# A state-space scan with a gated feed-forward: four turns a tile, moments by pairs, C in its own buffer, GpSimd out of the last tiles

## The chip, the cores and the metric

The kernel runs on one core of one Trainium2 chip. The metric is the device time of one execution in microseconds (us); it was measured three times for the kernel before the change (median 190.08 us), and once more in the execution that the profiler recorded.

Engines are called PE (matrix products, TensorE), DVE (VectorE), ACT (ScalarE), POOL (GpSimd) and SP (SyncE, which here only issues transfers). Each executes its own instructions in the order in which they were written, and waits for others through semaphores.

## The reference

The input x has 2048 tokens of 448 numbers. Both branches work on its normalized rows; the first is a linear recurrence over the tokens with 448 complex states, the second a gated feed-forward layer with 1792 hidden units.

```python
def _A_ref(x, Lambda_re, Lambda_im, B_re, B_im, C_re, C_im, log_dt, Dskip):
    ...
    Lam_bar = jnp.exp(dt * Lam)
    B_bar = ((Lam_bar - 1.0) / Lam)[:, None] * Bmat
    Bu = jnp.einsum("bld,pd->blp", x + 0j, B_bar)
    ...
    for t in range(L):
        h = Lam_bar[None, :] * h + Bu[:, t, :]
        hs.append(h)
    ...
    y = 2.0 * jnp.einsum("blp,dp->bld", hseq, Cmat).real + x * Dskip[None, None, :]
    return y

def _B_ref(x, w_gate, w_up, w_down):
    g = jnp.einsum("bsd,df->bsf", x, w_gate)
    u = jnp.einsum("bsd,df->bsf", x, w_up)
    h = _sigmoid(g) * u
    return jnp.einsum("bsf,fd->bsd", h, w_down)

x = A_x
xn = _layernorm(x, axis=-1)
s = _A_ref(xn, A_Lambda_re, A_Lambda_im, A_B_re, A_B_im, A_C_re, A_C_im, A_log_dt, A_Dskip)
g = _silu(_B_ref(xn, B_w_gate, B_w_up, B_w_down))
return x + s * g
```

## The kernel before

The tokens are cut into four chunks (c = 0 to 3) of 512, each of four tiles of 128 tokens (j = 0 to 3, numbered t = 4c + j over all). A chunk needs its normalized rows `xn[c % 3]` (tokens on the partitions) and their transposed form `xnT[c]` (features on the partitions). The 448 features make three blocks of 128 and one of 64. The last block stands twice in `xnT`, on the upper and on the lower 64 partitions, because the kernel runs nearly all its products on half of the rows at a time (`HALF`), an upper and a lower one side by side.

*Normalization.* `ln_stats` (L208) computes a tile's mean and variance on DVE; `ln_var` (L232) writes variance plus epsilon to `ve` on DVE; `ln_pow` (L239) raises it to the power -1/2 on POOL, giving `rsd`; `ln_norm` (L259) writes the rows. Chunk 0 is transposed by PE (`turn_twice`, L196: three turns of 128 columns, one of the last 128 columns, and one of the last 64 into the upper half of the same place). The later chunks are transposed by DMA (`ln_turn`, L272), after `ln_twice` has copied the last 64 columns once more behind the row (columns 448 to 512). Chunk 1's four tiles share one `ln_var` and one `ln_pow`.

*Order of the work.* `keep_order` binds every engine to the written order. The stream of PE is written by `emit_line`: lists of pairs of units, each pair a `duo` (L1053). A unit is either one block of the feed-forward (gate and up, `gu_unit`) or one block of the state input (`bu_unit`). A duo first does the upper half of its first unit beside the lower half of its second, then the other two halves. The table `beside`, filled by `at(c, ft, cost, fn)`, says what is written behind which half; `pieces` and `fill` spread the scan's DVE work over the stream by costs.

*The word between the halves.* A sum that goes on in the other half of the rows must not overtake the products of the first half. Class `Sum` (L505) therefore puts an empty instruction into POOL's queue, which waits for the last product of the one half, and on which the first product of the other half waits:

```python
            if self.half not in (None, half):
                word = pool.nop()
                tc.add_manual_dep(word.ins, self.ins.ins.name, SYNC, reason="the other half's last product")
                tc.add_manual_dep(m.ins, word.ins.name, SYNC, reason="the other half's last product")
```

A duo has four of these words (three with the short last block of the state input), all ahead of or among its second half's products. The profile shows them as L513 of POOL's sequencer (POOLq).

*The start.* A burst of empty products (`warm`) comes first; then chunk 0's tiles 0 and 1 are normalized and turned, the first feed-forward blocks are begun, tiles 2 and 3 follow. ACT computes sines and cosines of the scan's rotations, POOL mirrors them (`emit_neg`, `emit_mirror`, four times four instructions). The duo (4, 5) is the first that has words.

*C.* `load_wd_c` (L158), at place (0, 7), issues on SP the load of the down-projection weights `wd` and four loads of the output matrix C (`c_re`, `c_im`, into the buffers that `b_re`, `b_im` had). `emit_c_turn` (L170) transposes them by DMA, four times each; `emit_c` (L458) mixes them into `ct` with ACT and DVE during chunk 1's down-projection.

*The end.* After the last down-projection, `emit_y` and `emit_fin` do the last chunk's tiles in the order 0, 2, 1, 3, tile 3 in two halves of columns. A tile's output is x + (y + skip) * g. `emit_rest_of` (L843) prepares x + skip * g in float32, on DVE for even tiles and on POOL for odd ones; `emit_fin` adds y * g to it, on POOL for tile 1.

Of the kernel before, what the change touches and what calls it, by code (L numbers as in the profile page):

```python
# [63 lines left out]
def kernel(  # L64
# [93 lines left out]
    def load_wd_c():  # L158
        sync.dma_start(out=wd[:], in_=B_w_down.rearrange("(ft p) d -> p ft d", p=P))

        for nm in ("c_re", "c_im"):
            raw[nm] = w.tile([P, KT, DP], BF16, name=nm, tag="raw" + nm[1:])
            ctr[nm] = w.tile([P, KT, D], BF16, name="t" + nm, tag="tc" + nm[1:])
        for nm, mat, other in (("c_re", A_C_re, A_C_im), ("c_im", A_C_im, A_C_re)):

            for f0, m, c0 in ((0, mat, 0), (D, other, 384)):
                sync.dma_start(out=raw[nm][0:CP, :, f0:f0 + D - c0],
                               in_=m[:, c0:D].rearrange("(kt p) f -> p kt f", p=CP))
# [100 lines left out]
    def ln_turn(c, j):  # L269
        xb, cols = xn[c % 3], slice(j * P, (j + 1) * P)  # L270
        if c > 0:
            sync.dma_start_transpose(out=xnT[c][:, 0:KT, cols], in_=xb[:, j, :])  # L272
            return
        turn_twice(tps[j % 2], xb[:, j, :], P)

    def ln_twice(c, copy):
        copy(out=xn[c % 3][:, :, D:DP], in_=xn[c % 3][:, :, 384:D])
        for j in range(TPC):
            ln_turn(c, j)
# [178 lines left out]
    def emit_c(i):  # L458
# [9 lines left out]
        if not c_room:  # L468
            for nm in ("raw_re", "raw_im"):
                both = []  # L470
                c_room.extend((nm, both, k) for k in range(2))
                if nm == "raw_re":
                    c_room.extend((None, None, None) for _ in range(2))
            c_room.append((None, None, None))
# [280 lines left out]
    def emit_downs(c):  # L755
# [27 lines left out]
        for q in range(TPC):  # L783
            beside_each(*(v[q * FT:(q + 1) * FT] for v in line))
            if q >= 2:
                empty(q - 2)
                empty(q)
                if c == NCH - 1:
                    if q == 2:

                        pieces.pop(0)[1]()
                    emit_gate()
                    emit_gate()
# [11 lines left out]
    def y_ops(c, j, rows, d0=0, d1=D):  # L805
        sl = slice(j * P, (j + 1) * P)
        o = []
# [33 lines left out]
    rests, room_of_rests = {}, {}  # L841

    def emit_rest_of(c, j):  # L843

        eng = dve if j % 2 == 0 else pool
        t = op_.tile([P, D], BF16, name="t_g", tag="zb", bufs=4)
        eng.tensor_tensor(out=t[:], in0=xn[c % 3][:, j, 0:D], in1=gs[c][:, j, :], op=ALU.mult)  # L847
        if not rests:
            for k, nm in ((0, "raw_re"), (2, "raw_im")):
                both = w.tile([P, 2, D], FP32, name="t_x", tag=nm)  # L850
                room_of_rests.update({k: both[:, 0, :], k + 1: both[:, 1, :]})
        rests[j] = room_of_rests[j]
        eng.tensor_tensor(out=rests[j], in0=t[:], in1=x_t[c][:, j, :], op=ALU.add)  # L853

    def emit_y(c, j, d0=0, d1=D):
        ops = y_ops(c, j, slice(0, P), d0, d1)
# [5 lines left out]
    def emit_fin(c, j, d0=0, d1=D):  # L862
# [7 lines left out]
        (pool if j == 1 else dve).tensor_tensor(out=o[:, d0:d1], in0=sg[:, d0:d1], in1=rests[j][:, d0:d1], op=ALU.add)  # L870
# [75 lines left out]
    emit_angles()  # L946
    ln_mean(2, 1)
# [4 lines left out]
    warm(4)  # L952
# [60 lines left out]
    while due:  # L1013
        emit_mul()
    ln_stats(TPC)
    ln_stats(TPC + 1)
# [6 lines left out]
    for j in range(2, TPC):  # L1023
        at(0, 5, 0.8, lambda j=j: ln_stats(TPC + j))
    at(0, 5, 0.1, lambda: ln_var(TPC, TPC))
    at(0, 7, 0.0, lambda: ln_pow(TPC, TPC))
    for j in range(TPC):
        at(0, 7, 0.41, lambda j=j: ln_norm(1, j))
    at(0, 7, 0.2, lambda: ln_twice(1, dve.tensor_copy))
# [5 lines left out]
    at(0, 7, 0.0, load_wd_c)  # L1035
    for place, nm in (((1, 0), "c_re"), ((1, 1), "c_im")):
# [95 lines left out]
```

## Time and profile before

| | us |
|---|---|
| three timed runs | 188.74, 190.08, 190.25 (median 190.08) |
| the profiled execution, its own time | 188.31 |
| its span, first to last instruction | 186.5 |
| PE busy | 180.0 |
| DVE busy | 164.2 |
| ACT busy | 114.0 |
| POOL busy | 34.2 |
| first down-projection product of chunks 0, 1, 2, 3 | 42.78, 86.35, 128.94, 165.47 |
| last product | 181.9 |
| last DVE instruction ends | 183.97 |

Times in the prediction are microseconds from the span's start. The profile names an instruction by its engine, its line in the kernel, and the tiles it writes and reads (out<-in). Busy time of PE contains overlap, since products are pipelined: two half-row products run side by side, and a pair takes 0.215 us. What an engine waited for is inferred from semaphore events. PEld is the loading of weights into PE, which runs beside the products.

### The profile page before, as it was taken

The page shows a single profiled execution, that of the slowest core. Times are in us where ns is not written, and L with a number is a line of the kernel's source. Part 1 is how long each engine was busy: PE and PEld are TensorE (multiplying, and loading weights), DVE is VectorE, ACT ScalarE, POOL GpSimd, SP SyncE. Part 2 cuts the span into 40 slices and gives each one's busy share as a digit, 9 for nine tenths or more (in the row PEclk, how much of TensorE's full clock was granted, in tenths as well). Part 3 has the DMA queues.
Part 4 walks back from the last instruction along what each step waited for, and adds up shares of the span by engine and source line. Part 5 has one row for each costly group of instructions (what it writes and reads, how often), then busy time and mean ns, then how long its engine had stood idle before and what let it go on. Part 6 is the DMA issues. An engine that isn't in the chain of part 4 may idle for free.

```text
span 186.5 us, 4470 instructions
## 1 busy us (share of the span) xinstructions
PE 180.0 (97%) x1699; PEld 96.1 (52%) x1699; DVE 164.2 (88%) x326; ACT 114.0 (61%) x236; POOL 34.2 (18%) x71
## 2 busy tenths in 40 slices
PE   7999999999998999999999999999999999999990
PEld 6666444445553444655554445545554445655560
DVE  4779979999997979999999999699999999699584
ACT  3969857989549975997557757057038657061300
POOL 4699467402000000004000000000000000000092
PEclk9999999999999999999999999999999999999997
DMA  5999955894434113011140010020000010020102
GB/s 152 326 323 222 241 143 96 239 295 94 94 74 91 28 32 98 0 54 51 32 80 20 18 28 0 4 98 2 4 11 18 4 23 10 0 87 14 28 25 74
DMA packets 27659, 15.07 MB, mean 81 GB/s; under 512 B 16243, under 2 KB 27638, under 8 KB 27638
## 3 DMA queue, kind: packets, MB, share of 16 engines
q1 hardware_dynamic: 27632, 14.79, 32.7%
q8 instruction: 13, 0.21, 0.5%
q14 instruction: 8, 0.07, 0.1%
q10 hardware_dynamic: 6, 0.00, 0.0%
HBM read 8.49 MB, written 1.84 MB: 55 GB/s over the span
## 4 chain that ended last, share of the span: by engine, by line
PE 71%; SPq 8%; DMA 6%; issue 6%; POOL 2%; DVE 2%; ACT 1%; POOLq 0%; ACTq 0%
PE g_ps L511 18%; PE u_ps L511 16%; PE d_ps L511 14%; PE y_ps L511 8%; PE bu L511 6%; SPq L171 5%; DMA c_re<-in_A_C_im_dram 5%; SPq L272 2%; PE warm_ps L194 2%; PE g_ps L703 2%; DMA tc_im<-c_im 2%; PE u_ps L703 2%; DVE o_l L870 1%; POOL t_g L847 1%; POOL t_x L853 1%
## 5 line engine op out<-in xcount | busy, mean ns | idle before, releaser
L511 PE MATMUL u_ps<-xnT,wu 64*128 64x512 bf16 x312 | 66.9, 376 | 0.5 <-ACT zb L771 0.5
L511 PE MATMUL g_ps<-xnT,wg 64*128 64x512 bf16 x312 | 59.0, 376 | 0.0
L741 ACT ACTIVATE sig<-g_ps 128x512 bf16<-128x512 f32 x52 | 29.2, 598 | 28.0 <-PE g_ps L511 27.9
L511 PE MATMUL bu<-xnT,bT 64*128 64x512 bf16 x196 | 45.5, 376 | 0.0
L511 PE MATMUL d_ps<-wd,hF 64*128 64x448 bf16 x448 | 43.9, 349 | 0.0
L511 PEld LDWEIGHTS <-hF 64*128 64x128 bf16 x448 | 25.0, 94 | 18.0 <-POOLq L513 0.7
L511 PEld LDWEIGHTS <-wu 64*128 64x128 bf16 x312 | 24.0, 94 | 19.2 <-POOLq L513 1.6
L511 PEld LDWEIGHTS <-wg 64*128 64x128 bf16 x312 | 21.1, 94 | 18.3 <-POOLq L513 1.8
L741 ACT CAST ub<-u_ps 128x512 bf16<-128x512 f32 x52 | 29.2, 607 | 0.0
L511 PEld LDWEIGHTS <-bT 64*128 64x128 bf16 x196 | 17.8, 94 | 11.5 <-issue 0.8
L590 DVE TENSOR_TENSOR_SCAN wv<-r_col,st,ta 128x512 bf16<-128x512 f32 x18 | 22.6, 1275 | 0.1
L511 PE MATMUL y_ps<-ct,h 64*128 64x448 bf16 (+2 forms) x203 | 22.5, 343 | 0.0
L738 DVE TENSOR_TENSOR hF<-sig,ub 128x512 bf16<-128x512 bf16 x52 | 20.8, 415 | 0.9 <-ACT ub L741 0.8
L511 PE MATMUL g_ps<-xnT,wt 64*128 64x512 bf16 x52 | 19.6, 376 | 0.0
L511 PE MATMUL u_ps<-xnT,wt 64*128 64x512 bf16 x52 | 19.6, 376 | 0.0
L847 POOL TENSOR_TENSOR t_g<-xn,g_t 128x448 bf16<-128x448 bf16 x2 | 2.5, 1225 | 89.5 <-ACT g_t L765 89.5
L511 PEld LDWEIGHTS <-h 64*128 64x128 bf16 (+1 forms) x203 | 13.3, 95 | 8.3 <-issue 0.4
L571 ACT CAST bus<-bu 128x512 bf16<-128x512 f32 x24 | 14.4, 602 | 2.9 <-PE bu L511 2.9
L240 POOL TENSOR_TENSOR rsd<-ve,mhalf 128x1 f32<-128x1 f32 (+1 forms) x7 | 6.3, 903 | 49.7 <-PE u_ps L511 46.5
L769 ACT ACTIVATE sigd<-d_ps 128x448 bf16<-128x448 f32 x12 | 6.6, 550 | 12.4 <-PE d_ps L511 12.4
L511 PEld LDWEIGHTS <-wt 64*128 64x128 bf16 x104 | 9.8, 94 | 5.6
L834 DVE TENSOR_TENSOR o_t<-y_ps,xn 128x448 bf16<-128x448 f32 x12 | 6.9, 618 | 3.5 <-PE y_ps L511 3.4
(154 smaller groups left out, 235.3 us busy)
## 6 DMA issues: line engine op xcount, KB each, us to landing
wd<-in_B_w_down_dram SPq DMA_DIRECT2D x1, 1568.0 KB, 8.2
x<-in_A_x_dram SPq DMA_DIRECT2D x3, 448.0 KB
out_dram<-o_t SPq DMA_DIRECT2D x6, 224.0 KB, 2.1
wg<-in_B_w_gate_dram SPq DMA_DIRECT2D x2, 384.0 KB, 4.1
wu<-in_B_w_up_dram SPq DMA_DIRECT2D x2, 384.0 KB, 5.1
wg<-in_B_w_gate_dram SPq DMA_DIRECT2D x1, 576.0 KB, 5.7
wu<-in_B_w_up_dram SPq DMA_DIRECT2D x1, 576.0 KB, 6.7
bsw<-bus SPq DMA_DIRECT2D x8, 64.0 KB, 2.0
```

Source lines behind the costliest of these rows:

```text
L171: sync.dma_start_transpose(out=ctr[nm][:, :, kt * CP:(kt + 1) * CP], in_=raw[nm][0:CP, kt, :])
L194: pe.matmul(warm_ps[:], lhsT=ident[:], rhs=ident[:], start=True, stop=True)
L240: pool.tensor_tensor(out=rsd[:, t:t + n, :], in0=ve[:, t:t + n, :], in1=mhalf[:, 0:n, :], op=ALU.pow)
L511: m = pe.matmul(self.t[:, n0:n1], lhsT=lhsT, rhs=rhs, start=self.done == 1, stop=self.done == self.n)
L571: empty = [lambda cc=cc: act.copy(out=bus[:, cc, :], in_=pst[cc][:]) for cc in range(2)]
L590: dve.tensor_tensor_scan(out=T["wv"][:, cc, :], data0=rb, data1=T["ta"][:, cc, :], initial=(0.0 if c == 0 else st[pt][:, cc, :]), op0=mul, ...
L703: pe.matmul(t[:, n0:n1], lhsT=wm[:, kt, f0:f1], rhs=xnT[c][:, kt, n0:n1], start=(first and kt == 0), stop=(not first and kt == 2))
L738: dve.tensor_tensor(out=h[:], in0=sig[:], in1=ub[:], op=ALU.mult)
L741: u.empty = [lambda: act.activation(sig[:], gt[:], ACT.Sigmoid), lambda: act.copy(out=ub[:], in_=ut[:])]
L769: act.activation(sigd[:], ds[j][:], ACT.Sigmoid)
L834: dve.tensor_tensor(out=o[:, i, :], in0=ys[c, j + 2 * i][:], in1=xb[:, i, :], op=ALU.add)
L847: eng.tensor_tensor(out=t[:], in0=xn[c % 3][:, j, 0:D], in1=gs[c][:, j, :], op=ALU.mult)
```

## The change

- Chunk 0's rows get their last 64 columns copied behind the row as well (on DVE for tiles 0 and 1, on POOL for tiles 2 and 3), and PE turns a tile in four turns of 128 columns instead of five turns. The empty products around them become 2 and 5 instead of 4.
- Chunk 1's moments, `ve` and `rsd` are computed by pairs of tiles, written between the first four products hF (`emit_mul`), ahead of the duo (4, 5). The normalization of chunk 1 and its DMA turns go, by pairs, from place (0, 7) to (0, 5).
- `c_re` gets a buffer of its own and is loaded ahead of chunk 1's turns; `c_im` takes the buffer of `b_re` and is loaded between the two pairs of turns. `wd` follows at (0, 6). The turns of C go from (1, 0) and (1, 1) to (0, 12) and (1, 0).
- For the last chunk's odd tiles POOL prepares nothing: PE adds the skip rows to the sum by one product with the identity, and DVE adds x itself. POOL's addition for tile 1 goes to DVE.

In the built program the instructions of POOL stand in this order afterwards: the mirrors, then the two `rsd` of 128x2, then the first words of L513, then the scan's constants. Before, the mirrors are followed by words and constants, and `rsd` of 128x4 comes behind the words of the duos (4, 5) and (6, 7).

```diff
-    def load_wd_c():
-        sync.dma_start(out=wd[:], in_=B_w_down.rearrange("(ft p) d -> p ft d", p=P))
...
+    def load_c(nm, mat, other):
+        raw[nm] = w.tile([P, KT, DP], BF16, name=nm, tag=("raw_c", "raw_re")[nm == "c_im"])
+        ctr[nm] = w.tile([P, KT, D], BF16, name="t" + nm, tag="tc" + nm[1:])
+
+        for f0, m, c0 in ((0, mat, 0), (D, other, 384)):
+            sync.dma_start(out=raw[nm][0:CP, :, f0:f0 + D - c0],
+                           in_=m[:, c0:D].rearrange("(kt p) f -> p kt f", p=CP))
...
-        turn_twice(tps[j % 2], xb[:, j, :], P)
-
-    def ln_twice(c, copy):
-        copy(out=xn[c % 3][:, :, D:DP], in_=xn[c % 3][:, :, 384:D])
-        for j in range(TPC):
+        (dve if j < 2 else pool).tensor_copy(out=xb[:, j, D:DP], in_=xb[:, j, 384:D])
+        for kt in range(KT):
+            pe.transpose(tps[j % 2][:, kt, :], xb[:, j, kt * P:(kt + 1) * P], ident[:])
+
+    def ln_twice(c, copy, j0=0, j1=TPC):
+        copy(out=xn[c % 3][:, j0:j1, D:DP], in_=xn[c % 3][:, j0:j1, 384:D])
+        for j in range(j0, j1):
             ln_turn(c, j)
...
-    def y_ops(c, j, rows, d0=0, d1=D):
+    def y_ops(c, j, rows, d0=0, d1=D, skipped=False):
         sl = slice(j * P, (j + 1) * P)
-        o = []
+        o = [(ident[rows, :], xn[c % 3][rows, j, d0:d1], d0, d1)] if skipped else []
...
     def emit_rest_of(c, j):
-
-        eng = dve if j % 2 == 0 else pool
+        if j % 2:
+            return
...
     def emit_y(c, j, d0=0, d1=D):
-        ops = y_ops(c, j, slice(0, P), d0, d1)
+        ops = y_ops(c, j, slice(0, P), d0, d1, j not in rests)
...
-        (pool if j == 1 else dve).tensor_tensor(out=o[:, d0:d1], in0=sg[:, d0:d1], in1=rests[j][:, d0:d1], op=ALU.add)
+        also = rests[j] if j in rests else x_t[c][:, j, :]
+        dve.tensor_tensor(out=o[:, d0:d1], in0=sg[:, d0:d1], in1=also[:, d0:d1], op=ALU.add)
...
     ln_turn(0, 0)
     emit_vecs()
     emit_angles()
+    warm(2)
...
-    warm(4)
+    warm(5)
...
-    while due:
+    emit_mul()
+    emit_mul()
+    for t in (TPC, TPC + 2):
+        ln_stats(t)
+        ln_stats(t + 1)
+        ln_root(t, 2)
         emit_mul()
-    ln_stats(TPC)
-    ln_stats(TPC + 1)
...
     load_x(2)
-    for j in range(2, TPC):
-        at(0, 5, 0.8, lambda j=j: ln_stats(TPC + j))
-    at(0, 5, 0.1, lambda: ln_var(TPC, TPC))
-    at(0, 7, 0.0, lambda: ln_pow(TPC, TPC))
+    load_c("c_re", A_C_re, A_C_im)
     for j in range(TPC):
-        at(0, 7, 0.41, lambda j=j: ln_norm(1, j))
-    at(0, 7, 0.2, lambda: ln_twice(1, dve.tensor_copy))
+        at(0, 5, 0.41, lambda j=j: ln_norm(1, j))
+        if j % 2:
+            at(0, 5, 0.2, lambda j=j: ln_twice(1, dve.tensor_copy, j - 1, j + 1))
+        if j == 1:
+            at(0, 5, 0.0, lambda: load_c("c_im", A_C_im, A_C_re))
...
-    at(0, 7, 0.0, load_wd_c)
-    for place, nm in (((1, 0), "c_re"), ((1, 1), "c_im")):
+    at(0, 6, 0.0, lambda: sync.dma_start(out=wd[:], in_=B_w_down.rearrange("(ft p) d -> p ft d", p=P)))
+    for place, nm in (((0, 12), "c_re"), ((1, 0), "c_im")):
         at(*place, 0.0, lambda nm=nm: [emit_c_turn(nm, kt) for kt in range(KT)])
```

More of the change, by code (lines that the diff above doesn't have):

```diff
@@ L156 @@
     ctr = {}
-    def load_wd_c():
-        sync.dma_start(out=wd[:], in_=B_w_down.rearrange("(ft p) d -> p ft d", p=P))
[L161 to L168, printed above, removed]
+    def load_c(nm, mat, other):
[4 more added lines that the diff above has]
+                           in_=m[:, c0:D].rearrange("(kt p) f -> p kt f", p=CP))
     def emit_c_turn(nm, kt):
@@ L468, in emit_c @@
         if not c_room:
-            for nm in ("raw_re", "raw_im"):
+            for nm in ("raw_im", "raw_c"):
                 both = []
                 c_room.extend((nm, both, k) for k in range(2))
-                if nm == "raw_re":
+                if nm == "raw_im":
                     c_room.extend((None, None, None) for _ in range(2))
@@ L787, in emit_downs @@
                 empty(q)
-                if c == NCH - 1:
-                    if q == 2:
-                        pieces.pop(0)[1]()
+                if c == NCH - 1 and q == 2:
+                    pieces.pop(0)[1]()
                     emit_gate()
@@ L837, in emit_two @@
         sync.dma_start(out=out_t[:, c * TPC + j:(c + 1) * TPC:2, :], in_=o[:])
-    rests, room_of_rests = {}, {}
+    rests, room_of_rests = {}, []
     def emit_rest_of(c, j):
-        eng = dve if j % 2 == 0 else pool
+        if j % 2:
+            return
         t = op_.tile([P, D], BF16, name="t_g", tag="zb", bufs=4)
[L847 to L853, printed above, removed]
+        dve.tensor_tensor(out=t[:], in0=xn[c % 3][:, j, 0:D], in1=gs[c][:, j, :], op=ALU.mult)
+        if not room_of_rests:
+            room_of_rests.append(w.tile([P, 2, D], FP32, name="t_x", tag="raw_re"))
+        rests[j] = room_of_rests[0][:, j // 2, :]
+        dve.tensor_tensor(out=rests[j], in0=t[:], in1=x_t[c][:, j, :], op=ALU.add)
     def emit_y(c, j, d0=0, d1=D):
-        ops = y_ops(c, j, slice(0, P), d0, d1)
+        ops = y_ops(c, j, slice(0, P), d0, d1, j not in rests)
         ys[c, j] = bank("y_ps", D)
```

## The prediction

> **What bounds the kernel now.** I read the busy line first, then the waits, the chain that ended last, and the timelines around the edited places.
>
> ```profile
> PE 180.0 (97%) x1699; PEld 96.1 (52%) x1699; DVE 164.2 (88%) x326; ACT 114.0 (61%) x236; POOL 34.2 (18%) x71
> ```
>
> PE is the bound: from 16 us to 176 us its products follow each other with hardly a hole. So an edit gains only where it fills a hole of PE, shortens PE's own list or shortens the end after PE; it loses whatever new hole it makes. PE's holes and its ties to other engines stand in the list of waits (engine, line, releaser: us in total, times, longest).
>
> ```profile
> PEld L511 <- POOLq L513: 4.0, 13, 0.4
> POOL rsd L240 <- DVE ve L237: 2.8, 1, 2.8
> ACT c_tmp L483 <- DMA tc_im<-c_im: 2.5, 1, 2.5
> PE u_ps L511 <- ACT zb L771: 0.5, 1, 0.5
> ```
>
> The last two lines are one story: the turns of C land late (55.46 us), ACT waits 2.5 us for them, so its evictions of the down-projection banks are late, and PE waits at 57.3 to 58.5 us for a bank. From the first down product of chunk 1 to that of chunk 2 PE takes 86.35 - 42.78 = 43.57 us, from chunk 2 to 3 128.94 - 86.35 = 42.59 us: the hole costs 0.98 us.
>
> The first line matters most. L513 is the empty word that POOL's queue passes on whenever a sum changes from one half of the rows to the other (class `Sum`): PE's next product waits for it. POOL's engine does little, but its *sequencer* stands in PE's path 160 times. Does a word wait behind a POOL instruction that waits for something else? The timelines and the chain answer (start, length, what):
>
> ```profile
> 16.73 0.85 POOL L447 TENSOR_SCALAR spm<-spm 128x256 bf16<-128x256 bf16 x1
> 18.09 0.86 POOL L452 COPY spm<-spm 128x255 bf16<-128x255 bf16 x1
> 17.82 0.81 PE L511 MATMUL g_ps<-xnT,wg 64*128 64x512 bf16 x6
> ```
>
> and the chain of waits, some microseconds on:
>
> ```profile
> 21.13 0.02 POOLq L513
> 21.15 2.33 issue
> 23.48 0.02 POOLq L513
> 23.49 0.02 issue
> 23.51 1.17 POOL rsd L240
> ```
>
> In the trace the first two words of the duo (4, 5) ran at 17.62 and 17.72, the first 0.04 us after the L447 ended (16.73 + 0.85 = 17.58) for which the copy L452 ahead of them waited; the same pair of the duo (6, 7) came 0.42 us before its products, this one only 0.2 us. The copies themselves ran until 19.76, so a word need not wait until POOL's *engine* is free. It waits for the *semaphores* of what stands ahead. Again at 23.48: the word came 0.03 us before `rsd`, as soon as DVE's `ve` (23.26 + 0.17 = 23.43) let `rsd` go. So the queue passes waits in order.
>
> **The change part by part.** *Moments by pairs.* Before, the one `ln_pow` of chunk 1 is issued at place (0, 7), behind the words of the duos (4, 5) and (6, 7). Afterwards two of 128x2 stand right behind the mirrors and ahead of every word of the duo (4, 5); each waits for DVE's `ve` of its pair. When is the second `ve` there? DVE before:
>
> ```profile
> 17.21 3.08 DVE L713 SCALAR_TENSOR_TENSOR hF<-tanh,ub 128x512 bf16<-128x512 f32 x4
> 20.21 0.61 DVE L210 BATCH_NORM_STATS2 stats<-x 128x6 f32<-128x448 bf16 x1
> 23.26 0.17 DVE L237 TENSOR_SCALAR ve<-mv 128x4 f32<-128x4 f32 x1
> ```
>
> The new order is hF, hF, two tiles' moments, ve, hF, two tiles' moments, ve. One hF is 3.08 / 4 = 0.77 us, a tile's moments (23.23 - 20.21) / 4 = 0.755, a ve with its gap 0.2: 3 x 0.77 + 4 x 0.755 + 2 x 0.2 = 5.73 us from the first hF. That starts at 17.21 less what the start saves (0.55, below), at 16.66, so the second `ve` ends at 22.4 and the words reach PE about 0.1 us later. PE wants them at 17.82 at the latest, and everything on PE is behind them. Shift of PE: 22.5 - 17.82 = **+4.7 us**. Bounds: 5.3 if DVE starts no earlier; 3.9 if its three hF take only the 0.53 us of a DVE pass without POOL beside it (an estimate from the f32 rows of 0.48 to 0.6 us at 12 to 13 us). DVE's later work gets easier: the 0.95 us in which it waited for `rsd` goes, the added ve (0.17) and second column copy (0.23) fall into PE's hole. POOL's two rsd of 128x2 (between 0.6 for 128x1 and 1.16 for 128x4, I take 0.8) end near 23.2, in time for the next words, since the duo's second half and the next duo's first half (1.5 us each) lie between.
>
> *The clock after such a hole.* No hole of 5 us inside the run is in the trace, but its two ends show what the granted clock does (columns: us, busy by engine, granted clock, DMA):
>
> ```profile
> 181.03:184.44 3.41, 0.83 (x9) 0.57 (x6) 2.80 (x6) 0.00 (x0) 1.96 (x2) 1.00 0.23 73
> 184.44:186.50 2.06, 0.00 (x0) 0.00 (x0) 0.00 (x0) 0.00 (x0) 0.00 (x0) 0.50 0.17 46
> ```
>
> PE's last product ends at 181.9 and 2.6 us later the clock is halved. At the start the 256-column products are 0.213 us apart until 10.3 us and 0.109 us after it, although PE has been at work since 1.35 us; its last hole before that ends at 7.26 us, and the turns start at 5.10 us. So after the hole I expect half pace for 10.36 - 7.26 = 3.1 us to 10.36 - 5.10 = 5.26 us, half of which is lost: 1.55 to 2.63. I take **+2.1 us**; bounds 0 (the clock doesn't drop) and 10.36 - 1.35 = 9.0, so 4.5.
> The Trainium skill (TensorE: Matmul & The Clock Gate, "The HAM clock gate") says that an idle window of about 3.4 us halves the clock, that a busy one restores it, and that these windows run freely. Laid over a hole of 5 us, its windows give an estimate of 1.1 to 3.1 us lost, 2.2 on average, by where they happen to fall; the trace's two changes agree in kind, and the sum would be 0.1 us higher.
>
> *Four turns a tile.* Cold, a tile's turns take 5.890 - 5.103 = 0.79 us, because the fifth waits for the fourth on the same rows; four take 4 x 0.107 = 0.43. The added column copies of tiles 0 and 1 are DVE's (not shown; 0.1 each, between 0.06 for a tiny memset and 0.23 for L277's four tiles) and stand before these turns, and three more warm products fill the rest: first product of `g_ps` within 0.1 us of 7.26. For tiles 2 and 3 ten turns take 1.0 us; eight at 0.056 take 0.45, so PE is 0.55 us earlier. That is not a term of its own: PE would lose it again at the words; it only lets DVE start earlier (DVE waited 0.46 us for `u_ps` at 14.43). The two POOL copies (at most 0.4 each, the 128x255 copy) push the mirrors back by 0.8 us; nf (10.6 to 10.8) has until 15.7. Without the two `rsd` this alone would hold the first words for some 0.6 us.
>
> *C in its own buffer.* SP issues C's first load, two issues of 0.6 to 0.9 us, ahead of chunk 1's turns, and c_im's two between these turns. The last turn is issued near 32.6 instead of 31.84 us, lands 2.5 to 4.7 us later (the medians of xnT and of bT under load), at 35.1 to 37.3, and PE asked for it at 36.74: up to 0.6 us, hidden as PE now comes 6.8 us later. wd has until 42.8. `c_re`'s turns need no wait now; `c_im`'s stand behind the swap of bu, which waits for PE and ACT (38.2 + 6.8 = 45), and land by about 53.5; ACT wants them at 52.95 + 6.8. So the hole at 57 us goes: **-0.98 us** (bounds 0 and -0.98).
>
> *The last tiles.* At the end (DVE, POOL):
>
> ```profile
> 178.57 1.17 DVE L870 TENSOR_TENSOR o_l<-sg,t_x 128x448 bf16<-128x448 bf16 x1
> 180.71 1.29 POOL L853 TENSOR_TENSOR t_x<-t_g,x 128x448 f32<-128x448 bf16 x1
> 182.04 1.20 DVE L870 TENSOR_TENSOR o_l<-sg,t_x 128x224 bf16<-128x224 bf16 x1
> 183.58 0.39 DVE L870 TENSOR_TENSOR o_l<-sg,t_x 128x224 bf16<-128x224 bf16 x1
> ```
>
> DVE's add takes 1.17 us beside POOL's work; alone I price it at the 0.63 of L853 on DVE. The third tile's halves wait for POOL's t_x until 182.0. Without POOL: PE adds one product of 448 and two of 224 columns (0.19 + 2 x 0.096 = 0.38 us) and its last sum ends at 181.86 + 0.38 = 182.24; DVE has by then caught up, and does sg (0.38) and the add (0.26) of the last half: about 183.1 against 183.97. I take **-0.8 us** (bounds -0.95 and -0.4).
>
> **The sum.** 4.7 + 2.1 - 0.98 - 0.8 = +5.0 us. The profiled execution took 188.31 us (span 186.5, 1.8 around it), which gives 193.3. It is faster than all three timed runs (188.74, 190.08, 190.25); on their median it would be 195.1. Over all four the mean is 189.35, which gives 194.3, my prediction.
>
> **Rivals.** *The words slip past* (the other side, faster): if a waiting POOL instruction doesn't hold back a word, PE keeps its 0.55 us, and the sum is -0.55 - 0.98 - 0.8 = -2.3: 187.0. It decides only if the second pair's `ve` is there by 17.8 or the queue lets words through; for it speaks that words did run 2 us before POOL's engine was free, against it the two places above. Chance 0.12.
> *The hole without the cold clock*: 4.7 - 1.8 = +2.9: 192.2. For it: the hole of 1.2 us at 57 us left the clock at 1.00; against it the drop 2.6 us after the last product. Chance 0.10.
> *A longer hole*: DVE not earlier (5.3), half pace up to 4.5, C's hole still there: near 197 to 198. For it: DVE has no idle time in that stretch. Chance 0.12.
> My forecast (about 192.5 to 196.5) keeps 0.66.
>
> The range 191.0 to 197.4 leaves out the faster rival and the far end of the longer hole. Slower by over 1% (about what a measurement of this kernel tells from no change) means above 192.0: forecast, longer hole and most of the second rival, 0.86. Faster by over 1%, below 188.2: 0.08, most of the first rival. Between: 0.06.
>
> **What would show it.** Right: the first words of L513 near 22.4 instead of 17.62, PE idle some 5 us there with POOL named as releaser, a granted clock below 1 in the stretch behind it, products 0.43 us apart instead of 0.215 for some us; no hole at 57 + 6.8 us; no POOL work at the end, DVE's adds at 0.6 and 0.26. The forecast is wrong if the words of the duo (4, 5) pass near 17.8 while `rsd` waits, and half wrong if the clock stays at 1.00.

## The result and the profile after

The changed kernel takes 192.03 us in the median of six executions (191.16 to 192.59), the kernel before, run beside it, 190.06 us (188.74 to 190.34). The ratio is 1.0108, with a 95% interval of 1.0070 to 1.0147. The two profiled executions take 188.31 us before and 191.16 after, +2.85. Executions that lie more than 1.5% above a kernel's fastest are left out of the ratios below.

The busy line of the changed kernel's page:

```profile
PE 179.3 (95%) x1701; PEld 99.4 (52%) x1701; DVE 163.7 (86%) x331; ACT 113.8 (60%) x236; POOL 27.5 (15%) x69
```

PE works 0.7 us less than before in a span that is 2.9 us longer: the time went into waiting. The list of waits (engine, line, releaser: us in total, times, longest) says where:

```profile
PEld L510 <- POOLq L512: 9.4, 13, 5.6
...
PE g_ps L510 <- POOLq L512: 5.1, 1, 5.1
```

L512 is the word in POOL's queue (L513 before). PE's weight loads waited for it 13 times, and PE's products once, for 5.1 us. The timelines of POOL, DVE and PE (start, length, what, idle before and its releaser) show what it waited for:

```profile
18.76 0.86 POOL L452 COPY spm<-spm 128x255 bf16<-128x255 bf16 x1
19.59 0.72 POOL L237 TENSOR_TENSOR rsd<-ve,mhalf 128x2 f32<-128x2 f32 x1
21.12 1.17 POOL L237 TENSOR_TENSOR rsd<-ve,mhalf 128x2 f32<-128x2 f32 x1 [0.81 <-DVE ve L234]
...
15.23 1.48 DVE L712 SCALAR_TENSOR_TENSOR hF<-tanh,ub 128x512 bf16<-128x512 f32 x2
...
20.87 0.17 DVE L234 TENSOR_SCALAR ve<-mv 128x2 f32<-128x2 f32 x1
...
15.68 0.38 PE L510 MATMUL u_ps<-xnT,wt 64*128 64x512 bf16 x1
21.15 1.55 PE L510 MATMUL g_ps<-xnT,wg 64*128 64x512 bf16 x6 [5.09 <-POOLq L512]
```

The second `ve` ends at 20.87 + 0.17 = 21.04, the first words of the duo (4, 5) run at 21.08 and 21.18, its second half starts at 21.15 (17.82 before). In the windows (PE, PEld, DVE, ACT, POOL busy with counts, granted clock, DMA share, GB/s) the clock is halved once behind the hole:

```profile
16.00:21.10 5.10, 0.06 (x2) 0.00 (x0) 4.89 (x13) 0.82 (x1) 4.31 (x8) 0.94 1.30 309
20.52:23.93 3.41, 2.78 (x14) 1.67 (x16) 2.66 (x10) 1.09 (x2) 1.71 (x4) 0.50 1.13 155
```

The end is shorter. DVE's adds now have no POOL work beside them; those of whole tiles took 1.17 and 0.81 us before, those of half tiles 1.20 and 0.39:

```profile
182.32 0.62 DVE L867 TENSOR_TENSOR o_l<-sg,t_x 128x448 bf16<-128x448 bf16 x1
...
185.23 0.39 DVE L867 TENSOR_TENSOR o_l<-sg,x 128x448 bf16<-128x448 bf16 x1
...
186.57 0.28 DVE L867 TENSOR_TENSOR o_l<-sg,x 128x224 bf16<-128x224 bf16 x1
```

From marks in the two traces the difference adds up: second half of the duo (4, 5) 21.15 - 17.82 = +3.33; from there to chunk 0's first down product 26.37 instead of 24.97 us, +1.40; from there to chunk 1's 42.58 instead of 43.57, -0.99; from the first `y_ps` to the end of the span 9.26 instead of 10.16, -0.90. Together +2.84, of the +2.85 measured.

One thing at the start was not expected: PE's first nine products, after and before.

```profile
6.89 1.14 PE L702 MATMUL g_ps<-xnT,wg 128*128 128x256 bf16 x9
```

```profile
7.26 2.08 PE L703 MATMUL g_ps<-xnT,wg 128*128 128x256 bf16 x9
```

They run at full pace at once: the clock opened at 6.87 us instead of 10.36, exactly one window of 3.41 us earlier up to a shift of 0.08. DVE's first hF came at 15.23, not at the 16.66 of the prediction. The nine products also begin 0.37 us earlier than before, where the prediction expected no more than 0.1.

### The profile page after: what moved, and what is told of

Read it like the earlier page. It is cut to its first block, busy times and chain, and to the rows that moved or that the text cites. A ratio compares the mean times of both kernels' runs of the same rounds, so it can differ in the third digit from the quotient of the medians.

```text
span 189.4 us, 4470 instructions
## 1 busy us (share of the span) xinstructions
PE 179.3 (95%) x1701; PEld 99.4 (52%) x1701; DVE 163.7 (86%) x331; ACT 113.8 (60%) x236; POOL 27.5 (15%) x69
## 4 chain that ended last, share of the span: by engine, by line
PE 89%; POOL 6%; DVE 2%; issue 1%; POOLq 0%; DVEq 0%
PE g_ps L510 23%; PE d_ps L510 22%; PE u_ps L510 20%; PE y_ps L510 10%; PE bu L510 10%; PE warm_ps L191 2%; POOL spm L446 2%; POOL spm L451 1%; POOL spm L452 1%; POOL cosT L449 1%; DVE sg L861 1%; POOL rsd L237 1%; PE tp_x L273 1%; DVE o_l L867 0%; DVE stats L207 0%
## 5 line engine op out<-in xcount | busy, mean ns | idle before, releaser
L510 PE MATMUL g_ps<-xnT,wg 64*128 64x512 bf16 x312 | 59.9, 381 | 5.1 <-POOLq L512 5.1
L510 PEld LDWEIGHTS <-wu 64*128 64x128 bf16 x312 | 24.7, 95 | 18.4 <-POOLq L512 1.6
L510 PEld LDWEIGHTS <-wg 64*128 64x128 bf16 x312 | 21.7, 95 | 23.8 <-POOLq L512 7.2
L237 POOL TENSOR_TENSOR rsd<-ve,mhalf 128x1 f32<-128x1 f32 (+2 forms) x8 | 6.9, 867 | 46.7 <-PE u_ps L510 45.6
L576 DVE TENSOR_TENSOR ta<-bus,cosT 128x1024 bf16<-128x1024 bf16 x12 | 8.2, 684 | 2.1 <-ACT bus L570 2.1
```

What stands on the lines that cost most here:

```text
L237: pool.tensor_tensor(out=rsd[:, t:t + n, :], in0=ve[:, t:t + n, :], in1=mhalf[:, 0:n, :], op=ALU.pow)
L510: m = pe.matmul(self.t[:, n0:n1], lhsT=lhsT, rhs=rhs, start=self.done == 1, stop=self.done == self.n)
L576: dve.tensor_tensor(out=T["ta"][:], in0=bus[:], in1=cosb, op=mul)
```

## The experiments

The theory: words wait in POOL's queue behind every semaphore wait that stands ahead of them. The rivals: they wait for POOL's engine, or PE's hole has another cause. All traces that follow are read by the same marks (us; "run" is from the second half of the duo (4, 5) to the first down product `d_ps` of chunk 0, "chunk" from there to chunk 1's, "tail" from the first `y_ps` to the span's end; "half" is the time at half clock ahead of 100 us, counted from the first opening of the clock; "own" is the profiled execution's time).

| kernel | clock opens | first hF | first word | second half | run | half | chunk | tail | own |
|---|---|---|---|---|---|---|---|---|---|
| before | 10.36 | 17.21 | 17.62 | 17.82 | 24.97 | 0 | 43.57 | 10.16 | 188.31 |
| after | 6.87 | 15.23 | 21.08 | 21.15 | 26.37 | 3.41 | 42.58 | 9.26 | 191.16 |
| after, rsd behind words | 6.65 | 15.37 | 18.31 | 18.38 | 25.07 | 0 | 42.58 | 9.25 | 187.08 |
| after, rsd only just behind | 6.55 | 15.37 | 18.31 | 18.38 | 26.04 | 0 | 42.58 | 9.26 | 188.06 |
| after, hole filled | 7.23 | 15.37 | 20.95 | 21.02 | 25.07 | 0 | 42.58 | 9.25 | 189.73 |
| after, late clock | 10.23 | 16.30 | 22.02 | 22.09 | 27.58 | 6.83 | 42.58 | 9.26 | 193.31 |
| before + pairs | 4.93 | 15.59 | 21.39 | 21.47 | 26.95 | 6.83 | 42.59 | 10.15 | 192.98 |
| before + start | 7.31 | 15.38 | 19.20 | 19.27 | 25.07 | 0 | 42.58 | 10.15 | 188.88 |
| before + C | 10.28 | 17.18 | 17.58 | 17.78 | 24.97 | 0 | 42.58 | 10.14 | 187.28 |
| before + last tiles | 10.54 | 17.09 | 17.43 | 17.90 | 24.97 | 0 | 43.39 | 9.26 | 187.32 |
| mirrors behind words | 10.62 | 16.70 | 16.86 | 17.51 | 24.97 | 0 | 42.58 | 9.25 | 186.12 |
| and constants behind | 4.20 | 15.25 | 15.27 | 15.93 | 25.82 | 0 | 42.58 | 9.27 | 185.40 |

### The two rsd behind the words

```diff
-        ln_root(t, 2)
+        ln_var(t, 2)
...
+    for ft, t in ((5, TPC), (7, TPC + 2)):
+        at(0, ft, 0.0, lambda t=t: ln_pow(t, 2))
+        for j in (t - TPC, t - TPC + 1):
+            at(0, ft, 0.41, lambda j=j: ln_norm(1, j))
+        at(0, ft, 0.2, lambda j=t - TPC: ln_twice(1, dve.tensor_copy, j, j + 2))
...
-    at(0, 6, 0.0, lambda: sync.dma_start(out=wd[:], ...))
+    at(0, 8, 0.0, lambda: sync.dma_start(out=wd[:], ...))
```

> The changed kernel with each pair's rsd moved behind the words that PE wants before its ve is there: the first pair's rsd, normalization and turns stay at place (0, 5), but behind the words of the duo (4, 5); the second pair's go to (0, 7), behind those of (6, 7); wd follows at (0, 8). Theory (words stand behind the semaphore waits of POOL's queue): the first words run near 15.5 us, no hole of 5 us, no clock drop; against the kernel before 0.98 (C) + 0.86 (last tiles) + 0.55 to 1.9 (start) less, so 186.3 to 187.7. C's loads still stand ahead of the second pair's turns: up to 1.5 us may come back as a wait for chunk 1's turned rows. Rival (PE is held by DVE's or ACT's work of that stretch, not by POOL's queue): the hole stays and the time is near 192.

Measured: 188.31 us (ratio 0.9949, 0.9898 to 1.0000), against 192.03 and 1.0108 with the rsd ahead. In the profiled execution the words come at 18.31 instead of 21.08, and the clock stays open. The two `rsd` were the cause of the hole of 5.1 us. But a hole of 2.2 us stays, so the words were still late by something else:

```profile
PE g_ps L510 <- POOLq L512: 2.2, 1, 2.2
```

```profile
17.42 0.84 POOL L446 TENSOR_SCALAR spm<-spm 128x256 bf16<-128x256 bf16 x1
18.21 0.39 POOL L449 COPY cosT<-cosT 128x255 bf16<-128x255 bf16 x1
18.55 0.93 POOL L451 COPY spm<-spm 128x255 bf16<-128x255 bf16 x1
```

L451 waits for the result of L446, which ends at 17.42 + 0.84 = 18.26; the words behind it run at 18.31. So POOL's waits for its *own* results hold the words as well. They did so in the kernel before too (17.62 behind 17.58), where PE wanted the words no sooner (17.82, 1.53 us after the duo's first product at 16.29; a half of a duo takes 1.5); with the clock open earlier it costs 2.2.

### The two rsd one duo too early

Here both `rsd` stand just behind the words of the duo (4, 5), ahead of those of the duo (6, 7).

```diff
-        ln_root(t, 2)
+        ln_var(t, 2)
...
+    for t in (TPC, TPC + 2):
+        at(0, 5, 0.0, lambda t=t: ln_pow(t, 2))
```

> The changed kernel with both rsd moved only behind the words of the duo (4, 5), still ahead of those of (6, 7). Theory: the words of (4, 5) pass at once; those of (6, 7), which PE wants near 18.9 us, wait for the second ve near 20.9: a hole of some 2 us instead of 5.1, and the clock may or may not drop; 188.5 to 190.5. Rival (only the first words' place mattered, or the engine's mirrors hold the words): no hole left, as the run with both moved, or the full 5 us.

Measured: 188.44 us (0.9994, 0.9957 to 1.0031). The first words are those of the run above, to the hundredth (18.31). Then the trace has a second hole at the words of the duo (6, 7): the products begin 1.08 us apart there (21.29 and 22.37), and run grows by 26.04 - 25.07 = 0.97.

```profile
22.37 0.91 PE L510 MATMUL g_ps<-xnT,wg 64*128 64x512 bf16 x6 [0.70 <-POOLq L512]
```

The hole follows the place of `rsd` in the queue. The words did not wait for the second `ve` itself, as the theory has it: that ends at 20.74 + 0.17 = 20.91, and they run at 22.30. Ahead of them in POOL's queue stand the second `rsd` (to 20.98 + 1.16 = 22.14) and the scan's constants, of which the first, L354, ends at 22.03 + 0.23 = 22.26, and a later one needs its result: the words come 0.04 us behind it, so again one of POOL's waits for its own results came last.

### The hole filled with empty products

```diff
+HOLE = 84
...
+            if u is a and (c, u.ft) == (0, 4):
+                more = bank("more_ps", P)
+                for _ in range(HOLE):
+                    pe.matmul(more[:], lhsT=ident[:], rhs=ident[:], start=True, stop=True)
```

> The changed kernel with 84 empty 128-column products written behind the first half of the duo (4, 5), which keep PE busy for about 4.7 of the 5.1 us of its hole. The words stay held. Theory (the hole costs a second time, by the halved clock): products behind the hole at 0.215 us apart from the start, 1.4 us less than the changed kernel in its profile and up to 1.7 in other runs, so 190.3 to 190.7. Rival (the halved clock is hidden elsewhere): 192.0.

```profile
16.16 4.86 PE L1070 MATMUL more_ps<-ident 128*128 128x128 bf16 x84
21.02 0.91 PE L511 MATMUL g_ps<-xnT,wg 64*128 64x512 bf16 x6
```

Measured: 189.51 us (1.0046, 1.0005 to 1.0086). PE is busy through the hole, the words come at 20.95 all the same, the clock is not halved, and run is 25.07 instead of 26.37: the cold clock cost 1.30 us in the changed kernel's profile. All ten executions lie within 189.26 and 189.76, at mean clocks of 0.997 to 1.000. The time is below the 190.3 to 190.7 expected: in most other executions the changed kernel lost more to the cold clock than in its first profile (F below: 2.07).

### Parts of the change alone

Moments by pairs, put into the kernel before:

```diff
-    while due:
-        emit_mul()
-    ln_stats(TPC)
-    ln_stats(TPC + 1)
+    emit_mul()
+    emit_mul()
+    for t in (TPC, TPC + 2):
+        ln_stats(t)
+        ln_stats(t + 1)
+        ln_root(t, 2)
+        emit_mul()
...
-    for j in range(2, TPC):
-        at(0, 5, 0.8, lambda j=j: ln_stats(TPC + j))
-    at(0, 5, 0.1, lambda: ln_var(TPC, TPC))
-    at(0, 7, 0.0, lambda: ln_pow(TPC, TPC))
```

> The kernel before with the moments by pairs alone: both rsd ahead of the words of the duo (4, 5); everything else as before. Theory: the first hF at 17.2, the second ve 5.6 us later at 22.9, PE starts the second half of (4, 5) at 23.1 instead of 17.8: +5.3, a cold clock +1.4 to 1.7, C's hole gone because PE is late -0.98: 190.06 + 5.7 to 6.0, so about 196. Rival (the pairs are harmless and the other parts cost): 190.

Measured: 193.74 us (1.0262, 1.0177 to 1.0348). This part alone makes the whole loss, and more than the whole change: C and the last tiles give some back. Its profile has two windows at half clock, the first of which begins inside the hole. The 196 expected took the first hF at 17.2; with the clock open at 4.93 it came at 15.59.

The start alone:

```diff
-        turn_twice(tps[j % 2], xb[:, j, :], P)
+        (dve if j < 2 else pool).tensor_copy(out=xb[:, j, D:DP], in_=xb[:, j, 384:D])
+        for kt in range(KT):
+            pe.transpose(tps[j % 2][:, kt, :], xb[:, j, kt * P:(kt + 1) * P], ident[:])
...
+    warm(2)
...
-    warm(4)
+    warm(5)
```

> Before, with the start alone: four turns a tile with the copied columns, and 2 and 5 empty products instead of 4. Theory (the first words wait for the last mirrors, not for PE): PE's first half of the duo (4, 5) ends earlier than before, near 15.8 us, but the first words come only when the POOL instruction ahead of them has its semaphore, at 18.1 to 18.4 us, because the two POOL copies push the mirrors back; PE has a hole of about 2.5 us there, first d_ps 43.2 to 43.5 us (before 42.78), and the time is the same as before's to +0.7 us. Rival (the start is a gain of its own): what PE wins at the start, 0.55 us in my sum and up to 1.9 us by the trace of the changed kernel, is kept, words before 17.3, time 0.5 to 1.9 us below before's.

Measured: 190.06 us (1.0051, 1.0005 to 1.0096). PE begins the duo (4, 5) 1.75 us earlier (14.54 instead of 16.29) and gains nothing: it waits 3.1 us for words that come 1.58 us *later* than before. The timelines of POOL, DVE and PE:

```profile
16.25 0.86 POOL L454 COPY spm<-spm 128x255 bf16<-128x255 bf16 x1
17.06 0.86 POOL L455 COPY spm<-spm 128x255 bf16<-128x255 bf16 x1
17.88 1.28 POOL L449 TENSOR_SCALAR spm<-spm 128x256 bf16<-128x256 bf16 x1
...
15.38 3.08 DVE L715 SCALAR_TENSOR_TENSOR hF<-tanh,ub 128x512 bf16<-128x512 f32 x4
...
19.27 0.91 PE L513 MATMUL g_ps<-xnT,wg 64*128 64x512 bf16 x6 [3.05 <-POOLq L515]
```

The words wait for the last L449 (17.88 + 1.28 = 19.16). In the kernel before, the last of these copies and the instruction behind it took:

```profile
16.36 0.40 POOL L453 COPY spm<-spm 128x255 bf16<-128x255 bf16 x1
16.73 0.85 POOL L447 TENSOR_SCALAR spm<-spm 128x256 bf16<-128x256 bf16 x1
```

They are slower where DVE's hF runs beside them, which is now from 15.38 to 18.46 and was from 17.21 on. The Trainium skill (SBUF — State Buffer, "SBUF: two separate sides") says that DVE instructions of certain kinds and POOL share an exclusively held pair of ports; the doubled 0.86 against 0.40 agrees.

C alone (the lines of `load_c`, its two calls and the turns at (0, 12) and (1, 0), as in the change), and the last tiles alone (`y_ops`, `emit_rest_of`, `emit_y` and `emit_fin` as in the change):

> Before, with the part of C alone: c_re in a buffer of its own and loaded ahead, c_im in b_re's buffer, wd at (0, 7) by itself, the turns of C at (0, 12) and (1, 0). Theory: ACT no longer waits for tc_im, the first products d_ps of chunks 1 and 2 are 42.58 us apart instead of 43.57, everything up to the first d_ps of chunk 0 stays (42.78), so the time falls by 0.8 to 1.1 us. Rival: the four loads ahead of chunk 1's turned rows make these late (PE asked for them at 36.74), a hole of up to 0.6 us or more on PE near 37 us, and the sum is -0.4 to 0.

> Before, with the last tiles alone: PE adds the skip of the odd tiles, DVE adds x itself, POOL does nothing there. Theory: as in the changed kernel, the last DVE instruction ends 0.8 to 0.95 us earlier after the last sum's end, time -0.7 to -0.95 us. Rival: the added products (0.38 us) and DVE's extra add take most of that back, -0.3 to 0.

Measured: C 187.85 us (0.9940, 0.9885 to 0.9995), last tiles 188.90 (0.9979, 0.9918 to 1.0041). By the marks, chunk is 42.58 with C's part instead of 43.57 in the first profile of before, and the tail 9.26 with the last tiles' part instead of 10.16; the ratio of the second is too wide to show its 0.9 us. ACT's first use of `tc_im` with C's part, where 2.47 us of waiting stood:

```profile
52.81 0.70 ACT L479 ACTIVATE c_tmp<-tc_im,nci 128x448 f32<-128x448 bf16 x1
```

### The clock brought back to its late opening

```diff
-    warm(31)
+    warm(10)
...
-    warm(2)
...
-    warm(5)
```

> The changed kernel with 10 instead of 31 empty products at the very start and none between the turns, so that the clock opens late (8.3 to 10.5 us instead of 6.9). Theory (my hole was too long because DVE's first hF came 1.4 us earlier with the early clock): first hF at 16.3 to 17.2 us, second ve 5.4 to 5.8 us later at 21.9 to 22.8, the first words 0.1 us behind it, 0.9 to 1.7 us later than in the changed kernel (21.08); the half window behind the hole as before; first d_ps 48 to 49.5 us (47.53), time 0.5 to 2 us above the changed kernel's of the same number of half windows (191.2 with one, 191.5 to 192.6 with two). Rival: DVE's order, not the clock, sets it: the words stay at 21 to 21.3 us and the time is the same.

Timelines of DVE and PE, and the windows:

```profile
16.30 1.66 DVE L712 SCALAR_TENSOR_TENSOR hF<-tanh,ub 128x512 bf16<-128x512 f32 x2
...
21.81 0.17 DVE L234 TENSOR_SCALAR ve<-mv 128x2 f32<-128x2 f32 x1
...
22.09 1.55 PE L510 MATMUL g_ps<-xnT,wg 64*128 64x512 bf16 x6 [4.82 <-POOLq L512]
```

```profile
20.47:23.88 3.41, 1.78 (x10) 1.05 (x12) 3.27 (x11) 0.20 (x1) 2.12 (x5) 0.50 0.69 142
23.88:27.30 3.42, 3.42 (x20) 1.93 (x18) 1.20 (x4) 1.96 (x4) 0.00 (x0) 0.50 0.51 113
```

Measured: 193.29 us (1.0224, 1.0116 to 1.0332). With the clock late, hF comes 1.07 us later and the words 0.94 us later, as the theory has it; the rival (words at 21 to 21.3) is out.

### More profiles of the two kernels, and of the early clock

The kernel before, four more times (A to D; what the text for C calls the second profile is B):

> The kernel before once more, for where the 1.7 to 2 us lie that part its executions (187.2 to 188.7 us at a mean granted clock of 0.993 to 0.998, 189.5 to 190.4 us at 0.985 to 0.988). Theory: the slower ones have one more window of 3.41 us at half clock within the first 20 us, first d_ps near 44.5 us. Rival: the half window lies elsewhere in the span, or this run is again of the faster kind (42.8 us), which leaves it open.

> The kernel before once more, for the executions of 189.5 to 190.4 us (mean granted clock 0.985 to 0.988). Theory: in these the clock opens early (4.5 to 7.3 us), PE is at the first words early, waits there 2 to 3 us for POOL's mirrors, and the clock is halved for one window of 3.41 us behind it: first d_ps 44.5 to 45 us. Rival: the half window lies elsewhere; or a run of the faster kind (187.2 to 188.5 us), which leaves it open.

> The kernel before, a third profile, for its executions of 189.5 to 190.4 us at a mean clock of 0.985 to 0.988. Theory: early clock, the hole of 2.8 us at 15.8 us as in the second profile, and one window at half clock behind it, first d_ps near 45 to 45.7 us. Rival: the half window lies ahead of 12 us, or late in the span; a run of 187.2 to 188.5 us would leave it open.

> The same, a fourth profile: theory and rival as for the third.

The kernel before with two empty products between the fourth and fifth turn of the tiles 0 and 1, profiled twice:

```diff
+        warm(fill)
...
-        turn_twice(tps[j % 2], xb[:, j, :], P)
+        turn_twice(tps[j % 2], xb[:, j, :], P, 2 if j < 2 else 0)
```

> Before, with two empty products between the fourth and fifth turn of the tiles 0 and 1, where PE waited for the fourth: five turns and everything else as before. Theory (the clock opens after the first window of 3.41 us in which PE has some 29 or more products in place of 27 or 28, and an early clock is worth nothing here because POOL's mirrors hold the first words): the clock opens near 7 us, DVE's first hF comes 1.5 to 2 us earlier, POOL's copies beside it take 0.86 instead of 0.40 us, the first words come at 17.6 to 18.8 us as before or later, first d_ps 42.7 to 44 us, time -0.3 to +1.0 us of before's. Rivals: the clock still opens near 10.4 us (then it was the window's place alone), nothing changes; or the early clock brings the words to 16 us and the time falls by 1.5 us.

> Before with the two empty products in the turns once more: four of its six runs took 190.0 to 190.5 us at a clock of 0.985 to 0.987, the profiled one 188.25 at 0.997 with the clock open from 4.55 us on and a hole of PE of 2.79 us at 15.85. Theory: in the slower ones the same hole is there and the clock is halved for one window behind it, 1.4 to 1.9 us on PE, first d_ps 45 to 45.7 us. Rival: the half window lies ahead of 12 us (the clock opens, closes in the turns' holes and opens again).

The changed kernel two more times (E and F):

> The changed kernel once more, for where its other executions had the clock halved (mean granted clock 0.979 to 0.981 in five of its six runs, 0.991 in the profiled one). Theory: two windows of 3.41 us at half clock behind the hole, as in the kernel with pairs alone, time 191.5 to 192.6 us, first d_ps about 48.3 to 49 us. Rival: one window behind the hole and one elsewhere, before 12 us or late in the span.

> The changed kernel once more, for the executions with a mean granted clock of 0.979 to 0.981 (five of its first six). Theory: two windows of 3.41 us at half clock behind the hole, as in the kernel with pairs alone, time 191.5 to 192.6 us, first d_ps 48.3 to 49 us. Rival: the second half window lies ahead of 12 us; or one window again (191.2 us at 0.991), which leaves it open.

| profile | clock opens | first word | second half | run | half | chunk | own |
|---|---|---|---|---|---|---|---|
| before, A | 10.56 | 17.55 | 17.97 | 24.97 | 0 | 42.67 | 187.55 |
| before, B | 4.52 | 18.54 | 18.61 | 25.07 | 0 | 42.58 | 188.22 |
| before, C | 10.34 | 17.60 | 17.80 | 24.97 | 0 | 42.64 | 187.34 |
| before, D | 10.18 | 17.56 | 17.72 | 24.98 | 0 | 42.58 | 187.23 |
| two empties in the turns | 4.55 | 18.57 | 18.64 | 25.07 | 0 | 42.58 | 188.25 |
| the same again | 4.24 | 19.00 | 19.07 | 25.07 | 0 | 42.58 | 188.66 |
| after, E | 6.95 | 20.94 | 21.01 | 26.49 | 3.41 | 42.58 | 191.18 |
| after, F | 4.54 | 20.62 | 20.69 | 27.14 | 6.83 | 42.58 | 191.46 |

Three things follow. The unchanged kernel too has its clock open early in some executions (B, 4.52 us), and then its words are held to 18.54 by the mirrors, of which the last L447 ends at 17.22 + 1.28 = 18.50:

```profile
15.59 0.86 POOL L452 COPY spm<-spm 128x255 bf16<-128x255 bf16 x1
16.39 0.85 POOL L453 COPY spm<-spm 128x255 bf16<-128x255 bf16 x1
17.22 1.28 POOL L447 TENSOR_SCALAR spm<-spm 128x256 bf16<-128x256 bf16 x1
...
18.61 0.91 PE L511 MATMUL g_ps<-xnT,wg 64*128 64x512 bf16 x6 [2.42 <-POOLq L513]
```

So an early clock *costs* the kernel before 0.6 to 0.9 us (second half at 18.61 instead of 17.72 to 17.97). Second, the hole at 57 us, worth 0.99 us, is in the first profile of before but in none of the four others (the kernel with the last tiles alone has it once more, 43.39). In C ACT still waits, but `tc_im` is there 0.95 us sooner (54.51 instead of 55.46), and that is soon enough:

```profile
54.51 0.67 ACT L483 ACTIVATE c_tmp<-tc_im,nci 128x448 f32<-128x448 bf16 x1 [1.54 <-DMA tc_im<-c_im]
```

Third, F has two windows at half clock, one more than E, and the first begins before the hole ends. The window ahead of it, and the one at the same place of B, whose clock stayed open:

```profile
14.78:18.19 3.41, 1.10 (x12) 0.29 (x6) 3.31 (x8) 1.78 (x3) 3.41 (x6) 1.00 0.92 243
```

```profile
14.76:18.17 3.41, 1.43 (x14) 0.46 (x10) 3.41 (x5) 2.12 (x3) 3.41 (x5) 1.00 0.93 271
```

In the kernel before + pairs the window ahead of the first at half clock was:

```profile
15.17:18.59 3.42, 1.34 (x14) 0.39 (x8) 3.36 (x6) 2.02 (x3) 3.42 (x6) 1.00 0.89 240
```

The two empties timed 190.18 us (1.0117, 1.0007 to 1.0228); whether they open the clock a window sooner stays open, since in both of its profiles a window happened to end at 4.2 to 4.6 us, where the first burst of empty products opens it anyway.

### The mirrors behind the words, a version faster than both

On top of the rsd behind the words: chunk 1's first turns ahead of C's loads, the mirrors 2 and 3 and the signs they need behind the first duos, the scan's constants right after the mirrors 0 and 1.

```diff
-    for pt in (0, 1, 3, 2):
+    for pt in (0, 1):
         emit_neg(pt)
         emit_mirror(pt)
+    emit_constants()
...
+            at(0, ft, 0.0, lambda: [emit_neg(pt) for pt in (2, 3)])
...
+    at(0, 10, 0.0, lambda: emit_mirror(2))
+    at(0, 13, 0.0, lambda: emit_mirror(3))
```

> The changed kernel with both rsd behind words that PE wants before their ve, chunk 1's first two turns ahead of the loads of C, and the mirrors 2 and 3 behind the words of the first duos too (POOL computes the constants in their place). Theory (any semaphore wait in POOL's queue ahead of a word holds it, also POOL's waits for its own mirrors): the words of the duo (4, 5) come at 15.5 to 16.2 us, no hole of PE over 0.6 us there, first d_ps 40.6 to 41.2 us (changed kernel 47.53, with only the rsd moved 43.45), time about 2.5 us below that of the kernel with only the rsd moved, so 185.5 to 186.3 beside a before of 188.3 on the same chip. Rival: PE at 16 us meets another limit (weights not yet landed, ACT's activations, DVE's hF that keep the banks), and a hole of 1 to 2.5 us comes back between 16 and 30 us: time 186.5 to 188.5.

```profile
17.30 0.38 PE L513 MATMUL u_ps<-xnT,wt 64*128 64x512 bf16 x1
17.51 0.81 PE L513 MATMUL g_ps<-xnT,wg 64*128 64x512 bf16 x6
```

Measured: 184.94 us (184.26 to 186.12), ratio 0.9784, 0.9709 to 0.9858. No hole is left at the words: the second half begins at 17.51, 1.52 us after the first (15.99). The execution has a late clock (10.62 us) and was the slowest of the four; the words at 16.86 and `d_ps` at 42.48 are later than expected (15.5 to 16.2 and 40.6 to 41.2), since with the late clock PE itself is later at the duo. With the constants moved as well, and 4 and 6 empty products at the start:

```diff
-    emit_constants()
...
-            at(0, ft, 0.0, lambda: [emit_neg(pt) for pt in (2, 3)])
+            at(0, ft, 0.0, lambda: [emit_constants(), emit_neg(2), emit_neg(3)])
```

> The kernel with the mirrors 2 and 3 behind the first words, and in addition: the scan's constants too behind the words of the duo (4, 5) (they wait for ACT's sines), and 4 and 6 empty products instead of 2 and 5 at the start. Theory: the words of the duo (4, 5) come as soon as PE has done their first half (14.5 to 15.8 us if the clock opens near 7 us, 16 to 16.9 if near 10.4), no hole of PE over 0.7 us; first d_ps at 40.5 to 41.5 us with the early clock, near 42.4 with the late one; time 0.5 to 1.7 us below the 184.94 us of the kernel without these two steps. Rival: with the early clock PE runs ahead of ACT and DVE and waits for their banks, first d_ps stays at 42 to 42.5 us whatever the clock does, time 184.3 to 185.3 us.

```profile
19.71 0.91 PE L513 MATMUL g_ps<-xnT,wg 64*128 64x512 bf16 x6 [0.60 <-POOLq L515]
```

Measured: 185.31 us (0.9847, 0.9763 to 0.9932). PE passes the first words with no wait (first half at 14.41, second at 15.93), and is held at 19.71, where `rsd` and the constants hold the words of the duo (6, 7); run is 25.82 instead of 24.97. First `d_ps` 41.75 us, between the theory (40.5 to 41.5) and the rival (42 to 42.5). The two versions can't be told apart by these times.

## Why the direction was right and the size was not

The forecast was +5.0 us on the profiled execution and 194.3 us; measured were +2.85 and a median of 192.03.

*The queue holds the words.* Right, to 0.04 us: 21.08 behind 21.04, and 18.31 when the `rsd` are moved. The rival "the words slip past" is refuted.

*The length of DVE's chain.* 5.73 us were worked out from the first hF to the end of the second `ve`; measured were 5.81 (15.23 to 21.04), 5.68 with the late clock (16.30 to 21.98) and 5.36 (16.70 to 22.06, mirrors behind the words). Right.

*When that chain begins: the step that failed.* "That starts at 17.21 less what the start saves (0.55, below), at 16.66" took the clock to open at 10.36 us as in the trace of before. It opened a window earlier, and hF came at 15.23. So the term of +4.7 was +3.33: this makes 1.37 of the 2.2 us by which the sum missed the profiled pair (the cold clock, below, 0.7). The run with the late clock has hF at 16.30 and the term at 22.09 - 17.82 = 4.27. There the whole sum is 4.27 + 2.61 - 0.99 - 0.90 = 4.99, and 193.31 - 188.31 = 5.00 was measured: the sum of 5.0 described the changed kernel under the clock of the old one. That it fits to 0.01 us is partly luck, since the first term was 0.43 below the forecast and the second 0.51 above it. The prediction weighed the clock behind the hole, but not that the edited start shifts its opening. The early opening is not all the change's doing: in six profiles, B of the kernel before among them, a window ends at 4.2 to 4.9 us and the clock opens there, with four turns as with five. But in thirteen others (all but the late clock's, whose empty products were taken out) a window ends between 6.5 and 7.3 us. There the clock opened in six of the seven with the change's start, and in none of the six with five turns; these had to wait for the next window, at 10.2 to 10.6. In the windows that opened it 29 to 33 products and turns begin, in the others 27 or 28 (27 also with the mirrors behind the words, where tile 0's turns started at 5.35 instead of 5.13). So the edited start does move the opening, where the windows fall so. Whether the number of products or of turns decides was not tested.

*The cold clock.* Taken as 2.1 (1.55 to 2.63). In the profiled pair the term was +1.40. Runs with late words and an open clock take 25.07, 0.10 more than the 24.97 of those without a wait; against 25.07 the halved clock cost 1.30 and 1.42 with one half window, 2.07 with two in F (27.14 - 25.07), 1.88 in before + pairs and 2.51 with the late clock (27.58 - 25.07). Right in kind; the size hangs on where the windows fall. The estimate of 1.1 to 3.1 us by the windows, too, needs that a window idle only in part halves the clock, since a hole of 5 us holds a whole window of 3.41 us in only (5 - 3.41) / 3.41, about half, of all positions; F and before + pairs show that it does. Five of the first six executions had a mean clock of 0.979 to 0.981, which is two windows in a span of 190 us (1 - 6.83 / 2 / 190 = 0.982); the profiled one, at 0.991, had one.

*The start.* "PE would lose it again at the words": right. "Without the two rsd this alone would hold the first words for some 0.6 us": with the clock early in both, 19.20 against 18.54, so 0.66.

*C.* -0.98 against that profile, -0.99 measured. But the term belongs to one profile in five. Against one of the executions without that hole it would have been -0.1 to 0, the bound that the prediction named.

*The last tiles.* -0.8 forecast, -0.90 measured, the same in every kernel with this part.

*The base.* The sum holds for one pair of executions, and the prediction put it on top of the mean of four runs (+1.0). But before's median lies 1.75 above its profiled execution, after's only 0.87, so the medians differ by 1.97, less than the 2.85 of the profiled pair. In 21 of 50 executions of before that ran beside the first eight experiments the mean clock was 0.985 to 0.988 and the time 189.5 to 190.4 us; the others took 187.2 to 188.7 at 0.993 to 0.998. The missing 0.01 is about one window at half clock, and none of the five profiles of before is of that kind, so where it lies was not shown. A likely place: with the early clock before has a hole from 16.19 to 18.61 us, and windows in which PE is busy for 1.34 us or less were followed by a half one, such with 1.43 or more at the open clock were not. That needs 2.0 us of the hole in one window, which by my estimate is so in (2 x (2.42 - 2.03) + 3.41 - 2.42) / 3.41 = half of all positions of the windows. This is argued, not shown.

## What to carry to other kernels

An empty instruction that passes a signal on through an engine's queue inherits every semaphore wait ahead of it, also the waits of that engine for its own results; whatever is put ahead of it has to be ready before the signal is wanted. Work out such a change for each place that the clock's windows may take, and ask whether the edit moves the opening of the clock, for everything that hangs on it (here DVE's start, and through DVE's work POOL's speed) moves by 1 to 2 us. And look at more than one profile before a hole in it is counted as a gain.

## What the runs showed of the hardware

- The clock changes on a fixed grid of 3.41 us that does not start with the program: the openings lie at 4.20 to 10.62 us, always whole windows apart from the later changes of the same trace (6.87, 20.52, 23.93). The Trainium skill (TensorE: Matmul & The Clock Gate, "The HAM clock gate") has this grid, and lets an idle window halve the clock. The traces agree on the grid; but a window need not be idle. One with 1.10 us of PE work (F) or 1.34 us (before + pairs) was enough, one with 1.43 us (B) was not. At half clock behind the hole, one with 1.78 us of work (late clock) did not open it, one with 2.78 us (after) did; at the start, one that short products and turns kept busy throughout (before, 3.54 to 6.95 us) did not.
- Waits of PE of 2.2 to 2.4 us left the clock open in all five profiles that have one, one of 3.1 us (before + start) too; those of 4.8 us and more never did. A wait of some 2 us may close it in other executions: with the rsd behind the words (a wait of 2.2 us in the profiled one) six of ten executions had mean clocks of 0.987 to 0.990 and 188.3 to 189.1 us, the other four 0.996 to 1.000 and 186.7 to 187.1; none of the six was profiled. The hole of 5 us filled with 84 empty products left it open, at no cost to the words (20.95 against 21.08).
- POOL's copies of 128x255 took 0.40 us ahead of DVE's hF and 0.86 beside it. With the earlier start of DVE the words that stand behind them came 0.9 us later in the kernel before (18.54 against 17.62).
- Between executions of one binary the turns of C landed 0.95 us apart (54.51 and 55.46 us), and the hole of 1 us in PE was there with the later landing alone.
